# Attention softmax step: where the transposes and the two parts of the tile before stand in the order of work

## The chip, the cores and the metric

The kernel runs on one core of a Trainium2 chip. The core has five engines with a queue each: PE (TensorE, matrix products), DVE (VectorE), ACT (ScalarE), POOL (GpSimd) and SP (SyncE, which here issues DMAs). An engine works through its queue in order; engines wait for each other by semaphores. The metric is the device time of one execution in microseconds (us).

## The reference

Three stages in float32:

```python
q_pool = q.reshape(B, H, S // 2, 2, D).mean(axis=3)        # B 2, H 8, S 1152, D 64
scores = scale * q_pool @ k.T
attn = exp(scores - max(scores)); attn /= sum(attn) + 1e-9
x = (attn @ v) as [1152 tokens, 512]
xn = x / sqrt(mean(x * x) + 1e-6) * rms_g
y = (silu(xn @ w_gate) * (xn @ w_val)) @ w_out             # 512 -> 1536 -> 512
h = y @ w_in2;  out = (h * tanh(softplus(h))) @ w_out2     # 512 -> 2048 -> 512
```

## The kernel before

To keep float32's precision with 16-bit matrix products, each operand is kept as a high part (the value rounded to float16) and a low part (what the rounding left), and products are summed over the parts.

The attention runs first, in 72 steps: 8 pairs of heads (the code's groups g) of 9 tiles each, a tile being 128 pooled query rows. `attn_step(n)` writes out, in the order of its calls, what each engine gets for step n. This order is final: the kernel runs under a manual schedule, so every engine takes its instructions in exactly the order in which the calls issue them, and the framework only adds the waits for data and for free buffers. One tile passes through these calls:

- `scores(n)` (L237): PE multiplies queries and keys, 6 matmuls of 384 columns into one of two PSUM buffers of tile `s`.
- `row_max(n)` (L259): DVE takes the maximum of each row out of PSUM (L262, written to tile `m`) and scales it (L263).
- `row_exp(n)` (L266): ACT computes the exponential of 1152 columns from PSUM into `e` (float32, three buffers), L269.
- The exponentials have to be transposed and split into high and low parts, as tile `et` (five buffers), to be the weights of the product with v. Columns are divided: the first 640 go by DMA, the last 512 by PE.
  - DMA way: `split_hi` (ACT, L282) and `split_lo` (POOL, L134 of the helper `lo_op`) make the parts as `hl` (four buffers); `flip` (L292) has SP issue a transposing DMA from `hl` into `et`.
  - PE way: `flip_pe` (L297) transposes four blocks of `e` into one PSUM tile `ep`, of which there is a single buffer; `part_hi` (ACT, L309) writes the high part into `et`; `part_lo` (DVE, L314 by way of L134) reads `ep` and the high part and writes the low part, after which `ep` is free.
- `attn_v(n)` (L318), five steps later (LAG): PE multiplies `et` and v into `av`, a single PSUM buffer that two tiles share; `attn_r` and `attn_x` (L343, L353) are four small DVE operations that scale the rows, run for about every second tile. For the last pair of heads of a batch, `rms_sum` adds a sum of squares on ACT (L449).

`each(n, engine)` (L654) spreads the preparation of the next pair of heads over the nine steps of this one. By the position j of a step within its nine: on POOL `kv_scale` of k at j = 0 and of v at j = 6 (L141), low parts and the work on q in the others; on ACT `kv_hi` at j = 1, 2, 7, 8 (L154) and `q_hi` at 5 (L178); on PE `kq_flip` at j = 3, 4, 6, 7, 8 (L198), transposes into the PSUM buffer that the scores of step n - 1 have left, and on DVE `kq_keep` (L203), which copies them out of it, so that the scores of step n + 1 can have that buffer; the loads are issued from ACT's queue. The last pair of heads (steps 63 to 71) has no such work.

From step 46 on the steps of the rms norm of the first batch are mixed in, one after each attention step; from step 57 on, at odd steps, weight jobs (`job_step`, L420), which turn loaded weights into two parts: one ACT operation, three DVE operations (L396, L398, L400), one ACT and one POOL operation. Then the two feed-forward stages follow, on PE above all.

The part of `attn_step` that the change touches stands at L695 to L715.

Of the kernel before, what the change touches and what calls it, by code (L numbers as in the profile page):

```python
# [40 lines left out]
def kernel(  # L41
# [71 lines left out]
    def load(w, g, i, eng=nc.scalar):  # L113

        if g >= NPR:
            return
        b, h0 = g // NP, 2 * (g % NP)
        if i == 0:
            nat[w, g] = nat_p.tile([128, 2, NJ, D] if w != "q" else [128, NTI, 2, D], F32, tag="nat", name=w + "n")
        t = nat[w, g]  # L120
        nm = NI * 128 * 2
        if w != "q":
            eng.dma_start(out=t[:, i], in_=(k if w == "k" else v)[b, h0 + i].rearrange("(p j) d -> p j d", j=NJ))
        elif i < 2:
            eng.dma_start(
                out=t[:, i * NI:(i + 1) * NI], in_=q[b, h0 + i, 0:nm, :].rearrange("(p i r) d -> p i r d", i=NI, r=2))
        else:
            for e in range(2):
                eng.dma_start(out=t[e * TL:(e + 1) * TL, 2 * NI],
                                  in_=q[b, h0 + e, nm:, :].rearrange("(p r) d -> p r d", r=2))  # L130

    def lo_op(eng, out_, in_, s, hi):
        if isinstance(s, float) and s == 1.0:
            eng.tensor_tensor(out=out_, in0=in_, in1=hi, op=ALU.subtract)  # L134
        else:
            eng.scalar_tensor_tensor(out=out_, in0=in_, scalar=s, in1=hi, op0=ALU.mult, op1=ALU.subtract)  # L136

    def kv_scale(w, g):

        t = nat[w, g].rearrange("p h j d -> p (h j d)")  # L140
        nc.gpsimd.tensor_scalar(out=t, in0=t, scalar1=QK_S if w == "k" else V_S, scalar2=None, op0=ALU.mult)  # L141

    def kv_hi(w, g, e):
        if e == 0:
            if w == "k":
                cvt["k", g] = cv_p.tile([128, 2 * NJ, 2 * D], F16, tag="khl", name="khl")
            else:
                t = kq_p.tile([128, 2 * NJ, 2 * D + 2], F16, tag="vv", name="vv")
                nc.gpsimd.memset(t[:, :, 2 * D:2 * D + 1], 1.0)
                vvt[g] = t  # L150
        t = (cvt["k", g] if w == "k" else vvt[g])[:, e * NJ:(e + 1) * NJ, :]
        o = 0 if w == "k" else D
        sc = 1.0 if g else QK_S if w == "k" else V_S
        nc.scalar.activation(out=t[:, :, o:o + D], in_=nat[w, g][:, e], func=ACTF.Copy, scale=sc)  # L154

    def kv_lo(w, g, e):
        t = (cvt["k", g] if w == "k" else vvt[g])[:, e * NJ:(e + 1) * NJ, :]
        o = 0 if w == "k" else D
        sc = 1.0 if g else QK_S if w == "k" else V_S
        lo_op(nc.gpsimd if g else nc.vector, t[:, :, D - o:2 * D - o], nat[w, g][:, e], sc, t[:, :, o:o + D])  # L160
        if e == 1:
            del nat[w, g]

    def q_add(g):
        a = nat.pop(("q", g))
        s = cv_p.tile([128, NTI, D], F32, tag="qs", name="qs")
        (nc.gpsimd if g else nc.vector).tensor_tensor(out=s, in0=a[:, :, 0, :], in1=a[:, :, 1, :], op=ALU.add)
        cvt["s", g] = s
# [5 lines left out]
    def q_hi(g):  # L174

        t = cv_p.tile([128, NTI, 3, D], F16, tag="qhl", name="qhl")
        a = cvt["s", g]
        nc.scalar.activation(out=t[:, :, 0:3:2, :], in_=a.unsqueeze(2).to_broadcast([128, NTI, 2, D]), func=ACTF.Copy)  # L178
        cvt["q", g] = t
# [50 lines left out]
    def where(n):  # L230

        g, j = divmod(n, NTI)
        return g // NP, g, (j if g < NPR - 1 else (j - 1) % NTI)

    s_t, e_t, hl_t, et_t, av_t = {}, {}, {}, {}, {}

    def scores(n):  # L237
        b, g, j = where(n)
        kt = kqT[g][:, 0:2 * NJ, :]
        qt = kqT[g][:, 2 * NJ:, :]  # L240
        ps = ps_s.tile([128, SC, 512], F32, tag="s", name="s")
        heads = [(j % 2, j % 2 * NI + j // 2, 0, 128)] if j < 2 * NI else [
            (e, 2 * NI, e * TL, TL) for e in range(2)]
        per = SN // 128
        for c in range(SC):
            for e, slot, p0, m in heads:
                for w in range(2):
                    nc.tensor.matmul(  # L248
                        out=ps[p0:p0 + m, c, 0:SN],
                        lhsT=qt[:, w * NTI + slot, p0:p0 + m],  # L250
                        rhs=kt[:, e * NJ + c * per:e * NJ + (c + 1) * per, :].rearrange("p j t -> p (j t)"),
                        start=(w == 0),
                        stop=(w == 1),
                    )
        s_t[n] = ps
# [10 lines left out]
    def row_exp(n):  # L266
        ps, m = s_t.pop(n), mx.pop(n)
        e = e_p.tile([128, S], F32, tag="e", name="e")
        nc.scalar.activation(  # L269
            out=e.rearrange("p (c s) -> p c s", c=SC), in_=ps[:, :, 0:SN], func=ACTF.Exp,  # L270
            bias=m[:, 1:2], scale=s_scale)
        e_t[n] = e
        read[n] = ps
# [3 lines left out]
    def split_hi(n):  # L277

        if n < 0:
            return  # L280
        t = et_p.tile([128, 2, NB * 128], F16, tag="hl", name="hl", bufs=4)
        nc.scalar.activation(out=t[:, 0, :], in_=e_t[n][:, 0:NB * 128], func=ACTF.Copy)  # L282
        hl_t[n] = t

    def split_lo(n):
        e, t = e_t[n], hl_t[n]
        lo_op(nc.vector if n in LO_DVE else nc.gpsimd, t[:, 1, :], e[:, 0:NB * 128], 1.0, t[:, 0, :])

    def flip(n):
        t = hl_t.pop(n)  # L290
        r = et_p.tile([128, 2 * NJ, 128], F16, tag="et", name="et")
        nc.sync.dma_start_transpose(out=r[:, 0:2 * NB], in_=t.rearrange("p w s -> p (w s)"))  # L292
        et_t[n] = r
# [3 lines left out]
    def flip_pe(n):  # L297

        if n < 0:
            return  # L300
        e = e_t.pop(n)
        ps = ps_t.tile([128, PB, 128], F32, tag="t", name="ep")
        for s in range(PB):
            nc.tensor.transpose(out=ps[:, s, :], in_=e[:, (NB + s) * 128:(NB + s + 1) * 128], identity=idf)  # L304
        ep_t[n] = ps

    def part_hi(n):
        if n >= 0:
            nc.scalar.activation(out=et_t[n][:, 2 * NB:2 * NB + PB, :], in_=ep_t[n], func=ACTF.Copy)  # L309

    def part_lo(n):
        if n >= 0:
            r = et_t[n]
            lo_op(nc.vector, r[:, 2 * NB + PB:, :], ep_t.pop(n), 1.0, r[:, 2 * NB:2 * NB + PB, :])  # L314

    xb = {}
# [337 lines left out]
    def each(n, engine):  # L654

        g, j = n // NTI + 1, n % NTI
        if g >= NPR:
            return
        if engine == "load":
            if j in (0, 2):  # L660
                load("v", g, j // 2)
            elif j in (3, 4):
                load("k", g + 1, j - 3)
            elif j >= 6:
                load("q", g + 1, j - 6)
        elif engine == "act":
            if j in (1, 2):
                kv_hi("k", g, j - 1)
            elif j == 5:
                q_hi(g)  # L670
            elif j in (7, 8):
                kv_hi("v", g, j - 7)
        elif engine == "pool":
            if j in (0, 6):
                kv_scale("v" if j else "k", g)
            elif j in (1, 2):
                kv_lo("k", g, j - 1)
            elif j == 3:
                q_add(g)
            elif j == 4:  # L680
                q_scale(g)
            elif j == 5:
                q_lo(g)
            else:
                kv_lo("v", g, j - 7)
        elif j in FJ:
            f = FL[FJ.index(j)]
            if engine == "pe":
                kq_flip(read[n - 1], g, *f)
            else:  # L690
                kq_keep(g, f[0])
# [2 lines left out]

    def attn_step(n):  # L695
        scores(n)
        each(n, "pe")
        split_hi(n - 1)
        each(n, "act")
        row_max(n)  # L700
        each(n, "dve")
        row_exp(n)
        if n:
            split_lo(n - 1)
            flip(n - 1)
        each(n, "pool")
        each(n, "load")
        if n >= LAG:
            attn_v(n - LAG)
            attn_r(n - LAG)  # L710
            attn_x(n - LAG)
        flip_pe(n - 1)
        part_hi(n - 1)
        part_lo(n - 1)
        read.pop(n - 1, None)  # L715

    with tc.manual_schedule():
# [67 lines left out]
        for step in TAIL:  # L785
# [5 lines left out]
            else:  # L791
                n = NIT - LAG + int(step)
# [113 lines left out]
```

## Time and profile before

| what | value |
|---|---|
| time, median of 3 runs (lowest, highest) | 758.8 us (757.59, 759.13) |
| profiled execution: time, span | 757.44 us, 755.6 us |
| busy share of the span: PE, DVE, ACT, POOL | 83%, 62%, 51%, 47% |
| first and last exponential of the attention start at | 17.27 us, 332.73 us |
| mean granted TensorE clock | 0.959 of full |
| chain that ended last: PE, DVE, no visible wait, ACT | 41%, 31%, 13%, 9% |
| transposing DMAs `et` from `hl`: count, median from issue to landing | 72, 4.3 us |

The span is the time from the first to the last instruction of the profiled execution. "Busy" leaves out waiting; it is an average over stages that differ: in the attention no engine is full, while PE is nearly full later. A group of instructions in the profile has a source line, an engine, an operation and its tiles (written <- read); L134 is the helper for all low parts, so its groups are told apart by tile. An engine's idle time before a group is put down to what released it last. Times in the timeline are start and duration; on DVE, ACT and POOL the record of an instruction can overlap the next by about 0.1 us, so distances between starts are also used.

### The profile page before, as it was taken

The numbers are of one execution on the slowest core, as the hardware profiler recorded it, in microseconds if no ns is written. First come the engines' busy times: TensorE is split into PE (matmuls) and PEld (weight loads), VectorE is DVE, ScalarE is ACT, GpSimd is POOL, SyncE is SP. The second block draws the span as 40 slices with busy tenths as digits, with TensorE's granted clock in tenths as the row PEclk, the third lists the DMA queues.
The fourth block names the chain that finished last, engine by engine and source line by source line (L and its number), as shares of the span: only waits on it lengthen the run. The fifth ranks groups of instructions, "written<-read, shape, count | busy, mean of one in ns | idle before, by whom it ended". The sixth has DMA issues, their size and how long they took to land.

```text
span 755.6 us, 13340 instructions
## 1 busy us (share of the span) xinstructions
PE 629.6 (83%) x5232; PEld 441.1 (58%) x5232; DVE 465.9 (62%) x769; ACT 385.0 (51%) x654; POOL 355.6 (47%) x271
## 2 busy tenths in 40 slices
PE   3767677767657747578999999999999999999997
PEld 2555555545546545456777777777775555555553
DVE  5577777666677787865599998128939981111110
ACT  4766766676756655464555555304426652222321
POOL 2786878776868872320577777304504330000000
PEclk9799999999998986869999999999999999999999
DMA  5656666655658873431454555014514410000101
GB/s 176 139 123 136 125 129 133 142 108 120 134 119 186 139 150 79 111 70 36 120 159 150 159 168 162 7 56 140 168 57 144 167 53 28 15 1 1 43 0 43
DMA packets 143471, 79.25 MB, mean 105 GB/s; under 512 B 106288, under 2 KB 133936, under 8 KB 143408
## 3 DMA queue, kind: packets, MB, share of 16 engines
q1 hardware_dynamic: 132752, 63.00, 33.9%
q10 hardware_dynamic: 10656, 15.40, 8.0%
q8 instruction: 41, 0.67, 0.4%
q14 instruction: 22, 0.18, 0.1%
HBM read 50.07 MB, written 2.36 MB: 69 GB/s over the span
## 4 chain that ended last, share of the span: by engine, by line
PE 41%; DVE 31%; issue 13%; ACT 9%; POOL 3%; ACTq 1%; DMA 1%; SPq 0%; DVEq 0%; POOLq 0%
DVE m L262 10%; DVE c L398 6%; DVE et L134 5%; ACT et L309 5%; PE z L507 4%; PE z L509 4%; PE z L508 4%; PE po L644 4%; PE po L642 4%; PE po L643 4%; PE py L507 3%; PE py L509 3%; PE py L508 3%; DVE c L396 3%; ACT e L269 2%
## 5 line engine op out<-in xcount | busy, mean ns | idle before, releaser
L134 POOL TENSOR_TENSOR hl<-e,hl 128x640 f16<-128x640 f32 x71 | 101.1, 1424 | 92.9 <-ACT hl L282 71.3
L269 ACT ACTIVATE e<-s,m 128x1152 f32<-128x1152 f32 x72 | 87.8, 1220 | 104.1 <-DVE m L263 79.6
L248 PE MATMUL s<-kqT 128*128 128x384 f16 (+1 forms) x480 | 90.6, 350 | 43.3 <-DVE kqT L203 39.7
L134 DVE TENSOR_TENSOR et<-ep,et 128x512 f16<-128x512 f32 x72 | 49.8, 692 | 86.4 <-ACT et L309 86.4
L262 DVE TENSOR_REDUCE m<-s 128x1 f32<-128x1152 f32 x72 | 97.1, 1348 | 0.8 <-PE s L248 0.8
L331 PE MATMUL av<-vv,et 128*128 128x129 f16 (+1 forms) x720 | 79.8, 230 | 20.9 <-DVE x L366 17.2
L136 DVE SCALAR_TENSOR_TENSOR g<-mo,g 128x384 f16<-128x384 f32 x48 | 26.9, 562 | 100.5 <-ACT g L617 100.5
L248 PEld LDWEIGHTS <-kqT 128*128 128x128 f16 (+1 forms) x480 | 46.8, 106 | 71.5 <-issue 54.9
L331 PEld LDWEIGHTS <-et 128*128 128x128 f16 (+1 forms) x720 | 69.9, 105 | 29.8 <-issue 28.6
L398 DVE SCALAR_TENSOR_TENSOR c<-gx,c 128x512 int32<-128x512 int32 x68 | 79.1, 1164 | 2.3
L134 POOL TENSOR_TENSOR stretch<-c,stretch 128x512 f16<-128x512 f32 x40 | 51.4, 1284 | 58.9 <-ACT stretch L407 58.8
L333 PE MATMUL av<-vv,et 128*128 128x65 f16 (+1 forms) x720 | 77.6, 201 | 0.0
L400 DVE SCALAR_TENSOR_TENSOR c<-raw,c 128x512 int32<-128x512 int32 x68 | 75.1, 1105 | 2.3
L304 PE MATMUL ep<-idf,e 128*128 128x128 f32 x288 | 51.2, 305 | 26.2 <-DVE et L134 24.1
L333 PEld LDWEIGHTS <-et 128*128 128x128 f16 (+1 forms) x720 | 68.3, 105 | 1.0 <-issue 0.5
L134 POOL TENSOR_TENSOR h<-fo,h 128x288 f16<-128x288 f32 x48 | 48.8, 1017 | 42.3 <-ACT h L544 42.3
L507 PE MATMUL z<-y,w2i 128*128 128x384 f16 x192 | 62.6, 326 | 0.0
L509 PE MATMUL z<-y,w2i 128*128 128x384 f16 x192 | 62.6, 326 | 0.0
L508 PE MATMUL z<-y,w2i 128*128 128x384 f16 x192 | 62.6, 326 | 0.0
L611 ACT ACTIVATE mo<-z 128x384 f32<-128x384 f32 x48 | 23.2, 483 | 71.3 <-PE z L509 71.3
L507 PE MATMUL pv<-stretch 128*128 128x288 f16 x192 | 55.7, 290 | 2.4 <-DVE fo L537 2.3
L507 PE MATMUL pg<-stretch 128*128 128x288 f16 x192 | 55.9, 291 | 1.9 <-DMA stretch<-xh 1.9
(98 smaller groups left out, 1542.9 us busy)
## 6 DMA issues: line engine op xcount, KB each, us to landing
raw<-in_moe_w_out_dram SPq DMA_DIRECT2D x28, 512.0 KB, 3.4
raw<-in_moe_w_in_dram SPq DMA_DIRECT2D x16, 512.0 KB, 3.7
raw<-in_moe_w_gate_dram SPq DMA_DIRECT2D x8, 512.0 KB, 3.7
raw<-in_moe_w_val_dram SPq DMA_DIRECT2D x8, 512.0 KB, 3.6
vn<-in_v_dram ACTq DMA_DIRECT2D x14, 288.0 KB, 3.5
kn<-in_k_dram ACTq DMA_DIRECT2D x12, 288.0 KB, 3.4
qn<-in_q_dram ACTq DMA_DIRECT2D x12, 256.0 KB, 3.2
raw<-in_moe_w_gate_dram ACTq DMA_DIRECT2D x4, 512.0 KB, 5.0
```

The source lines that it names most:

```text
L134: eng.tensor_tensor(out=out_, in0=in_, in1=hi, op=ALU.subtract)
L248: nc.tensor.matmul(out=ps[p0:p0 + m, c, 0:SN], lhsT=qt[:, w * NTI + slot, p0:p0 + m], rhs=kt[:, e * NJ + c * per:e * NJ + (c + 1) * per, : ...
L262: nc.vector.tensor_reduce(out=m[:, 0:1], in_=ps[:, :, 0:SN], op=ALU.max, axis=AXL.XY, negate=True)
L269: nc.scalar.activation(out=e.rearrange("p (c s) -> p c s", c=SC), in_=ps[:, :, 0:SN], func=ACTF.Exp, bias=m[:, 1:2], scale=s_scale)
L304: nc.tensor.transpose(out=ps[:, s, :], in_=e[:, (NB + s) * 128:(NB + s + 1) * 128], identity=idf)
L331: nc.tensor.matmul(out=av[0:m, o0:o0 + 2 * D + 1], lhsT=et[:, z, p0:p0 + m], rhs=vr[:, 0:2 * D + 1], start=(jj == 0), stop=False)
L333: nc.tensor.matmul(out=av[0:m, o0 + D:o0 + 2 * D + 1], lhsT=et[:, z + (NB if jj < NB else PB), p0:p0 + m], rhs=vr[:, D:2 * D + 1], start=F ...
L398: nc.vector.scalar_tensor_tensor(out=c, in0=gi, scalar=-0x80000000, in1=c, op0=ALU.bitwise_and, op1=ALU.bitwise_or)
L400: nc.vector.scalar_tensor_tensor(out=c, in0=t[:, :, :, 0], scalar=29, in1=c, op0=ALU.logical_shift_right, op1=ALU.bitwise_or)
L507: nc.tensor.matmul(out=ps, lhsT=w0, rhs=x0, start=(i == 0), stop=False)
L508: nc.tensor.matmul(out=ps, lhsT=w0, rhs=x1, start=False, stop=False)
L509: nc.tensor.matmul(out=ps, lhsT=w1, rhs=x0, start=False, stop=(i == n - 1))
```

## The change

The calls of `attn_step` are put in another order; no instruction is added, removed or altered. Within step n, `flip_pe(n - 1)` moves from the end of the step to directly behind `scores(n)`, ahead of `kq_flip` and `attn_v` on PE. `split_lo(n - 1)` and `flip(n - 1)` are called earlier, which leaves POOL's and SP's order as it was. `part_hi(n - 1)` moves on ACT from behind the exponential of n to directly behind `split_hi(n - 1)`, ahead of `kv_hi` or `q_hi` and of the exponential of n. `part_lo(n - 1)` moves on DVE from the end of the step to directly behind `kq_keep`, ahead of `attn_r` and `attn_x`. The tile `e` is let go of in `part_lo` rather than in `flip_pe`, since `split_lo` now comes after `flip_pe`.

```diff
     def flip_pe(n):
...
-        e = e_t.pop(n)
+        e = e_t[n]
...
     def part_lo(n):
         if n >= 0:
             r = et_t[n]
+            del e_t[n]
             lo_op(nc.vector, r[:, 2 * NB + PB:, :], ep_t.pop(n), 1.0, r[:, 2 * NB:2 * NB + PB, :])
...
     def attn_step(n):
         scores(n)
+        flip_pe(n - 1)
         each(n, "pe")
         split_hi(n - 1)
+        if n:
+            split_lo(n - 1)
+            flip(n - 1)
+        part_hi(n - 1)
         each(n, "act")
         row_max(n)
         each(n, "dve")
+        part_lo(n - 1)
         row_exp(n)
-        if n:
-            split_lo(n - 1)
-            flip(n - 1)
         each(n, "pool")
         each(n, "load")
         if n >= LAG:
             attn_v(n - LAG)
             attn_r(n - LAG)
             attn_x(n - LAG)
-        flip_pe(n - 1)
-        part_hi(n - 1)
-        part_lo(n - 1)
         read.pop(n - 1, None)
```

## Rows read from the trace of the kernel before

**Rows 1.** Costliest groups: busy and mean ns of one, idle time before and its releaser.
```profile
L134 DVE TENSOR_TENSOR et<-ep,et 128x512 f16<-128x512 f32 x72 | 49.8, 692 | 86.4 <-ACT et L309 86.4
```

**Rows 2.** Chain of waits, one step: start us, us, what.
```profile
111.86 0.17 DVE m L263
112.11 0.37 ACT e L269
...
113.23 0.60 ACT et L309
113.85 0.69 DVE et L134
```

**Rows 3.** Timeline of DVE, the same step: start us, us, engine, line, operation.
```profile
111.93 0.68 DVE L203 COPY kqT<-s 128x1024 f16<-128x1024 f16 x1
112.53 0.15 DVE L350 TENSOR_SCALAR r<-av 128x2 f32<-128x2 f32 x1
...
113.24 0.29 DVE L366 TENSOR_TENSOR x<-av,r 128x128 f32<-128x128 f32 x1
...
114.45 1.35 DVE L262 TENSOR_REDUCE m<-s 128x1 f32<-128x1152 f32 x1
115.84 0.15 DVE L263 TENSOR_SCALAR m<-m 128x1 f32<-128x1 f32 x1
```

**Rows 4.** Timeline of ACT: exponentials of steps 0, 9, 18, 45, 63 and 71.
```profile
17.27 1.22 ACT L269 ACTIVATE e<-s,m 128x1152 f32<-128x1152 f32 x1 [1.80 <-DVE m L263]
...
52.15 1.22 ACT L269 ACTIVATE e<-s,m 128x1152 f32<-128x1152 f32 x1 [1.67 <-DVE m L263]
...
88.22 1.22 ACT L269 ACTIVATE e<-s,m 128x1152 f32<-128x1152 f32 x1 [1.67 <-DVE m L263]
...
200.82 1.22 ACT L269 ACTIVATE e<-s,m 128x1152 f32<-128x1152 f32 x1 [1.67 <-DVE m L263]
...
287.98 1.22 ACT L269 ACTIVATE e<-s,m 128x1152 f32<-128x1152 f32 x1 [1.80 <-PE av L333]
...
332.73 1.22 ACT L269 ACTIVATE e<-s,m 128x1152 f32<-128x1152 f32 x1 [1.67 <-PE av L333]
```

**Rows 5.** Windows: us, busy PE, PEld, DVE, ACT, POOL; PEclk, DMA share, GB/s.
```profile
52.00:88.00 36.00, 25.31 (x313) 19.45 (x312) 25.88 (x53) 24.66 (x32) 27.78 (x20) 1.00 0.61 132
...
288.00:333.00 45.00, 29.66 (x282) 22.58 (x280) 32.45 (x54) 23.37 (x35) 14.90 (x11) 0.80 0.42 94
```

**Rows 6.** Timeline of PE: attn_v, flip_pe, scores; scores and kq_flip.
```profile
105.70 0.22 PE L331 MATMUL av<-vv,et 128*128 128x129 f16 x1
...
106.64 0.66 PE L304 MATMUL ep<-idf,e 128*128 128x128 f32 x4
107.13 1.14 PE L248 MATMUL s<-kqT 128*128 128x384 f16 x6
...
112.66 1.14 PE L248 MATMUL s<-kqT 128*128 128x384 f16 x6 [1.39 <-DVE kqT L203]
113.63 0.61 PE L198 MATMUL s<-ident,qhl 128*128 128x128 f16 x8
```

**Rows 7.** Timeline of ACT: split_hi and a kv_hi that waits for POOL.
```profile
53.74 0.74 ACT L282 ACTIVATE hl<-e 128x640 f16<-128x640 f32 x1
55.08 0.68 ACT L154 ACTIVATE khl<-kn 128x576 f16<-128x576 f32 x1 [0.60 <-POOL kn L141]
```

**Rows 8.** Timeline of POOL: split_lo and kv_scale at position 0.
```profile
86.63 1.40 POOL L134 TENSOR_TENSOR hl<-e,hl 128x640 f16<-128x640 f32 x1 [1.61 <-ACT hl L282]
88.00 3.13 POOL L141 TENSOR_SCALAR kn<-kn 128x1152 f32<-128x1152 f32 x1
```

**Rows 9.** Timeline of DVE: first operations of two weight jobs, and a row maximum.
```profile
267.06 0.42 DVE L396 TENSOR_SCALAR c<-gx 128x512 int32<-128x512 int32 x1
...
290.33 1.40 DVE L396 TENSOR_SCALAR c<-gx 128x512 int32<-128x512 int32 x1
...
294.17 1.35 DVE L262 TENSOR_REDUCE m<-s 128x1 f32<-128x1152 f32 x1
```

## The prediction

> **What bounds the kernel now.** I read the page's costliest groups first, then the chain of waits inside the attention, then the timeline of each engine over one step. In the groups the reader is to see an engine that waits inside a step: DVE stands idle 86.4 us in front of its 72 part_lo, all of it until ACT's part_hi (L309) [rows 1]. The chain shows where that wait lies, in a ring: row maximum of tile n, exponential of n, then part_hi and part_lo of n - 1, then the row maximum of n + 1 [rows 2, 3]. No data asks for the middle link: row_max(n + 1) stands behind part_lo(n - 1) in DVE's order, and that waits for part_hi(n - 1), which stands behind exp(n) in ACT's order. From start to start the ring is 1.39 (row maximum to L263) + 0.25 (to the exponential) + 1.12 (to part_hi) + 0.62 (to part_lo) + 0.60 (to the next maximum) = 3.98 us [rows 2, 3]. A group of nine steps takes 88.22 - 52.15 = 36.07 us; steps 0 to 45 take 183.55, steps 45 to 63 87.16, steps 63 to 71 44.75 [rows 4]. In a stretch of about one group DVE is busy 25.9 us, ACT 24.7, POOL 27.8 and PE 25.3 [rows 5]. So nothing is full; order sets the time.
>
> **The change part by part.** No instruction is added or removed. POOL's and SP's own orders, each queue's loads and the transposing DMA stay in sequence; three things move.
>
> *part_lo(n - 1) on DVE*, from behind attn_x to in front of attn_r, and no longer behind exp(n). Its 86.4 us of idle time go, up to what is late next. DVE's own work per step, start to start, is 1.39 + 0.07 + 0.60 = 2.06 us, plus 0.60 for kq_keep (five steps of nine, the last shorter) and 0.95 for attn_r and attn_x (five of nine) [rows 3]: 2.9 us on the mean.
>
> *part_hi(n - 1) on ACT*, from behind exp(n) to in front of it. This adds a wait: exp(n) now stands behind part_hi(n - 1), which waits for PE's flip_pe(n - 1), which waits for exp(n - 1). split_hi follows exp directly and reads its output, so it starts 1.22 (the exponential's duration) + 0.04 (my estimate of a handoff) later, not 1.12. flip_pe takes 0.66 beside split_hi's 0.74 [rows 6, 7]. So part_hi starts 2.00 after its tile's exponential, the next exponential 2.48 after it at the earliest, with 0.58 more in four steps (kv_hi) and 1.08 more in one (q_hi).
>
> *flip_pe(n - 1) on PE*, in front of kq_flip and attn_v(n - 5), which now wait for exp(n - 1) as well, with scores(n + 1) and attn_x behind them. PE, start to start: scores 0.97, flip_pe 0.49, attn_v 0.87 to 0.94 (0.87 taken), kq_flip about 0.5 of its 0.61 [rows 6]. From scores' start to the row maximum I take their 1.14 + 0.10.
>
> What is late next I worked through one group, time zero at the row maximum of its step 0, the exponential before at -1.12 (the state that repeats).
> Steps 0 and 1: POOL sets it. split_hi ends at 0.98 (exp -1, + 1.36 behind two small load issues, + 0.74), POOL's split_lo takes 1.37 and kv_scale 3.13, to 5.5 [rows 8]; kv_hi on ACT waits for it, as it does by 0.60 us now [rows 7]. exp(1) starts at 6.13 instead of 4.37, which the row maximum before it would allow. Row maxima: 0, 2.74, 5.81.
> Step 2: exp(1) + 1.27 flip_pe, + 0.48 attn_v, + 0.87 scores, + 1.24: row maximum 3 at 9.99; exp(2), behind the second kv_hi, at 9.19.
> Steps 3 and 4: DVE sets it. Step 3: kq_keep waits for kq_flip until 11.63, then 0.60 + 0.61 + 0.95: 13.79. Step 4: 2.06 + 0.60 + 0.95 = 3.61: 17.40.
> Step 5: flip_pe(4) at 17.00, attn_v, scores: 19.59; exp(5) behind q_hi at 19.29.
> Step 6: kq_flip follows exp(5), kq_keep at 21.73: 23.89.
> Step 7: scores wait for kq_keep: 27.31; exp(7) waits for POOL's second kv_scale, 26.5.
> Step 8: part_lo waits for part_hi(7) until 29.12, + 0.61 + 0.95 = 30.68, with exp(8) at 29.56, so the state repeats. Group: 30.7 us against 36.07.
>
> Sum. Steps 0 to 45: 5 x 30.7 + 1.8 for the five sum-of-squares steps (ACT waits there for attn_x; now they cost about 4) = 155, against 183.5: 28 us. Steps 45 to 63: what now exceeds two groups, 87.16 - 72.1 = 15.0 us (rms steps, first weight jobs, mostly DVE's), stays; 2 x 5.4 = 10.7 us saved. Steps 63 to 71, no kq or kv work: DVE's 8 x 2.06 + 5 x 0.95 + three jobs of 3.84 [rows 9] = 32.8; I take 35, since TensorE's granted clock has a mean of 0.80 there [rows 5]: 9.5 us saved. Behind the loop about 0.5 us is won, and the rest moves rigidly: its first units need weights whose jobs run by step number in the loop. Together 48 to 49 us. The profiled execution took 757.44 us (span 755.6), so 709; the median of the runs shown is 758.8, 1.4 higher, which gives **711 us**.
>
> Bounds of what the trace doesn't show. exp beside row_max of the next tile, both reading PSUM: never so now. Nearest rows: kq_keep and attn_x read PSUM beside an exponential and take the 0.68 and 0.29 of other steps [rows 3], so I take 0; the other end is full serialisation, 1.22 per step (a rival below). Handoffs: 0.04 to 0.10 taken, from L263's end to the exponential's start, 0.1; at twice that the ring of two steps over PE has five of them, +0.2 per step, 14 us. Denser transfers: the DMA share of 0.61 [rows 5] becomes 0.72, et has four steps of slack; 0. Below nothing: fewer stalls may keep the clock up in steps 59 to 71, at most the 2 us I put in.
>
> A weight job's first DVE operation took 0.42 us in the first job and 1.40 in the third, which lasted 3.84 up to the next row maximum [rows 9]. The Trainium skill ("SBUF — State Buffer", Who interferes with whom) has the pair of ports that VectorE and GpSimd share as an exclusive lock: the second to issue waits for the whole of the other's instruction. The trace agrees for the jobs. A denser POOL would then hit the first job too, three operations by 1 us each, and four more operations of the rms steps: 718 by that rule, inside the forecast's own range; the sum above keeps the jobs' present cost.
>
> **The rivals.**
> *POOL's floor.* The waits overlap better than in my table and only POOL's 27.8 us per group are left [rows 5]: 3 us per group more over seven groups, 690. For: POOL queues four tiles deep. Against: kv_hi needs kv_scale a step later, already a wait now.
> *PE's ring is longer.* Every second-step handoff over exp, flip_pe, kq_flip, kq_keep, scores costs more than taken, 0.3 us per step: 71 x 0.3 = 21 us, 732. For: scores already wait for kq_keep in each such step. Against: that handoff is short now.
> *The gain is given back.* The order is new but the stage after the loop waits for the same weights: 757 to 760. Against: loads are issued by step number, DMA is at 0.61 [rows 5].
> *Slower: exp and row_max serialise.* Place: DVE and ACT on PSUM at once. Lengthening of y per step gives a group of 26.0 + 9y on DVE; it exceeds 36.07 from y = 1.12. At 1.22: 37.0, eight groups, 7 us more than before: 766. Against: rows 3, as said.
> *Slower: half clock.* PE's in-order work is 0.97 + 0.49 + 0.94 + 5/9 x 0.5 = 2.68 us per step at the full clock; with a share x of it at 1.2 GHz it is 2.68 (1 + x), over 3.98 from x = 0.5. At x = 0.6 it is 4.29, 71 x 0.31 = 22 us more than before: 781. For: a mean of 0.80 in steps 63 to 71, where PE idles under DVE's jobs. Against: 1.00 in the regular groups with PE busy 25.3 of 36 us [rows 5], and the same work will fill 30.7.
>
> **How the numbers follow.** Forecast 0.60 (702 to 722), POOL's floor 0.12, longer ring 0.17, given back 0.03, serialise 0.04, half clock 0.04. Leaving out the outer half of POOL's floor, the worst of the longer ring and the three last, the range is 694 to 738. A change under 0.2%, 1.5 us, can't be told from none. Faster: 0.60 + 0.12 + 0.17 = 0.89; same 0.03; slower 0.08.
>
> **What would show it.** Right: DVE's idle time before part_lo falls from 86.4 to under 15 us; row maxima run beside the exponential before; a regular group takes about 30.7 us with the long steps where kv_hi waits for kv_scale; exp waits for POOL in steps 1 and 7. Wrong: exponential or row maximum longer than 1.22 and 1.35; PE's clock below 1.00 in the regular groups; idle time before flip_pe or scores of over 1 us in most steps; or a stage after the loop that grew.

## The result and the profile after

The changed kernel takes **698.0 us** (median of 4 runs, 696.74 to 699.07) where the kernel before took 758.45 beside it (757.59 to 759.13): a ratio of 0.9203, with an interval of 0.9183 to 0.9223. Four more runs of the same kernel, in a later series, gave a median of 698.41 and again a ratio of 0.9203 (0.9171 to 0.9236). The forecast was 711, with a range of 694 to 738. The profiled execution took 697.47 us, with a span of 695.7 (before: 757.44 and 755.6); its mean granted TensorE clock is 0.983 of full (before: 0.959).

First the costliest groups of the kernel after: busy us and mean ns of one, then the idle time before them and what ended it. In this kernel part_lo stands at L134, the exponential at L269 and the row maximum at L262, as before; from L314 on, lines have moved down by one.

```profile
L262 DVE TENSOR_REDUCE m<-s 128x1 f32<-128x1152 f32 x72 | 97.2, 1350 | 12.5 <-PE s L248 12.2
L269 ACT ACTIVATE e<-s,m 128x1152 f32<-128x1152 f32 x72 | 87.4, 1214 | 20.3 <-DVE m L263 20.2
L134 DVE TENSOR_TENSOR et<-ep,et 128x512 f16<-128x512 f32 x72 | 49.4, 686 | 14.9 <-ACT et L309 14.5
```

DVE's idle time before part_lo fell from 86.4 us [rows 1] to 14.9, and neither of the two operations that now run beside each other on PSUM (row maximum and exponential, as at 83.50 and 83.75 us below) became longer by more than 2 ns of its mean.

The timeline of ACT of the kernel after (start, duration, operation; in brackets the idle time and what ended it) shows the exponentials of steps 0, 18, 27, 45, 63 and 71, and between them the new order as far as the exponential of step 19, with ACT's two waits for POOL in that group:

```profile
17.54 1.22 ACT L269 ACTIVATE e<-s,m 128x1152 f32<-128x1152 f32 x1 [1.81 <-DVE m L263]
...
79.37 1.22 ACT L269 ACTIVATE e<-s,m 128x1152 f32<-128x1152 f32 x1 [0.23 <-DVE m L263]
80.62 0.74 ACT L282 ACTIVATE hl<-e 128x640 f16<-128x640 f32 x1
81.34 0.60 ACT L309 ACTIVATE et<-ep 128x512 f16<-128x512 f32 x1
83.16 0.68 ACT L154 ACTIVATE khl<-kn 128x576 f16<-128x576 f32 x1 [1.23 <-POOL kn L141]
83.75 1.20 ACT L269 ACTIVATE e<-s,m 128x1152 f32<-128x1152 f32 x1
...
103.40 0.68 ACT L154 ACTIVATE vv<-vn 128x576 f16<-128x576 f32 x1 [1.16 <-POOL vn L141]
...
109.95 1.22 ACT L269 ACTIVATE e<-s,m 128x1152 f32<-128x1152 f32 x1 [0.39 <-DVE m L263]
...
172.77 1.22 ACT L269 ACTIVATE e<-s,m 128x1152 f32<-128x1152 f32 x1 [0.23 <-DVE m L263]
...
246.02 1.22 ACT L269 ACTIVATE e<-s,m 128x1152 f32<-128x1152 f32 x1 [0.62 <-DVE m L263]
...
276.43 1.21 ACT L269 ACTIVATE e<-s,m 128x1152 f32<-128x1152 f32 x1
```

Put beside [rows 4], the starts say where the 59.9 us of span went:

| stretch | before | after | saved | forecast to save |
|---|---|---|---|---|
| start to step 0 | 17.27 | 17.54 | -0.3 | 0 |
| steps 0 to 45 | 183.55 | 155.23 | 28.3 | 28 |
| steps 45 to 63 | 87.16 | 73.25 | 13.9 | 10.7 |
| steps 63 to 71 | 44.75 | 30.41 | 14.3 | 9.5 |
| from step 71 to the end | 422.9 | 419.3 | 3.6 | 0.5 |

A regular group (steps 18 to 27) takes 109.95 - 79.37 = 30.58 us; the table of the prediction said 30.7. The five groups of steps 0 to 45 took 29.90, 31.93, 30.58, 30.52 and 32.30 us (the last with the five sum-of-squares steps, for which the prediction had 32.5). The row maxima of that group, in the timeline of DVE after, test the table step by step:

```profile
77.74 1.35 DVE L262 TENSOR_REDUCE m<-s 128x1 f32<-128x1152 f32 x1
...
80.30 1.36 DVE L262 TENSOR_REDUCE m<-s 128x1 f32<-128x1152 f32 x1 [0.42 <-PE s L248]
...
83.50 1.35 DVE L262 TENSOR_REDUCE m<-s 128x1 f32<-128x1152 f32 x1
...
87.47 1.36 DVE L262 TENSOR_REDUCE m<-s 128x1 f32<-128x1152 f32 x1 [0.45 <-PE s L248]
...
91.38 1.35 DVE L262 TENSOR_REDUCE m<-s 128x1 f32<-128x1152 f32 x1
...
94.95 1.34 DVE L262 TENSOR_REDUCE m<-s 128x1 f32<-128x1152 f32 x1
...
97.13 1.36 DVE L262 TENSOR_REDUCE m<-s 128x1 f32<-128x1152 f32 x1
...
101.42 1.35 DVE L262 TENSOR_REDUCE m<-s 128x1 f32<-128x1152 f32 x1
...
104.84 1.36 DVE L262 TENSOR_REDUCE m<-s 128x1 f32<-128x1152 f32 x1 [0.66 <-PE s L248]
...
108.32 1.35 DVE L262 TENSOR_REDUCE m<-s 128x1 f32<-128x1152 f32 x1
```

From 77.74 on they come at 0, 2.56, 5.76, 9.73, 13.64, 17.21, 19.39, 23.68, 27.10 and 30.58; the table had 0, 2.74, 5.81, 9.99, 13.79, 17.40, 19.59, 23.89, 27.31 and 30.68.

What is late in the place of the old ring is read from the waits of the kernel after over the attention (17 to 285 us; total us, times, longest):

```profile
PE ep L304 <- ACT e L269: 42.6, 42, 3.3
...
DVE et L134 <- ACT et L309: 14.5, 15, 2.1
...
ACT et L309 <- PE ep L304: 10.9, 23, 1.6
ACT khl L154 <- POOL kn L141: 8.4, 6, 1.7
```

No one engine took over. PE waits 42 times, one microsecond on the mean, for the exponential (the link that the table had on purpose: flip_pe(n - 1) stands right behind the exponential), and ACT waits for POOL's scaling of k at the start of each group that prepares the next. In windows of the kernel after (us; busy PE, PEld, DVE, ACT, POOL; granted clock; DMA share; GB/s) all four are fuller than in [rows 5] without being full, the granted clock of steps 18 to 45 stays at 1.00, and that of the last nine steps rose from 0.80 to 0.94:

```profile
79.00:110.00 31.00, 25.38 (x322) 19.87 (x320) 26.42 (x55) 25.84 (x34) 28.45 (x20) 1.00 0.81 153
172.77:246.02 73.25, 54.09 (x634) 41.95 (x633) 65.57 (x121) 56.49 (x76) 67.15 (x45) 0.93 0.88 168
246.02:276.43 30.41, 22.69 (x273) 17.12 (x271) 27.77 (x54) 23.78 (x34) 14.62 (x12) 0.94 0.68 139
276.00:286.00 10.00, 8.85 (x105) 7.36 (x102) 5.11 (x16) 5.57 (x11) 1.40 (x1) 1.00 0.37 71
```

Of steps 9 to 45, those up to 18 are the exception. There the granted clock has a mean of 0.95 (0.62 from 53 to 57 us), where it was 1.00 before [rows 5], and one `scores` in PE's timeline takes nearly twice its usual 1.14 us:

```profile
55.20 2.11 PE L248 MATMUL s<-kqT 128*128 128x384 f16 x6
```

PE had waited 2.20 us just before, at flip_pe, for an exponential that stood behind POOL's scaling, and about 3 us of work then ran at the lower of the clock's two levels (1.2 instead of 2.4 GHz). The group took 31.93 us, 1.35 more than the next, and did so in the later series too. What lowered the clock is not shown: in the next group PE waited 1.94 us at the same place and the clock stayed at 1.00.

### The profile page after: what moved, and what is told of

It is laid out like the page before. It is cut to its first block, busy times and chain, and to the rows that moved or that the text cites. A ratio compares the mean times of both kernels' runs of the same rounds, so it can differ in the third digit from the quotient of the medians.

```text
span 695.7 us, 13395 instructions
## 1 busy us (share of the span) xinstructions
PE 611.0 (88%) x5232; PEld 430.4 (62%) x5232; DVE 460.0 (66%) x769; ACT 391.1 (56%) x654; POOL 357.5 (51%) x271
## 4 chain that ended last, share of the span: by engine, by line
PE 47%; DVE 20%; POOL 11%; issue 11%; ACT 8%; DMA 2%; SPq 0%; ACTq 0%; POOLq 0%; DVEq 0%
DVE c L399 6%; PE z L508 4%; PE z L510 4%; PE z L509 4%; PE po L645 4%; PE po L644 4%; PE po L643 4%; ACT e L269 3%; PE py L508 3%; PE py L510 3%; PE py L509 3%; POOL hl L134 3%; DVE m L262 3%; DVE c L397 3%; DVE c L401 2%
## 5 line engine op out<-in xcount | busy, mean ns | idle before, releaser
L134 POOL TENSOR_TENSOR hl<-e,hl 128x640 f16<-128x640 f32 x71 | 101.1, 1423 | 36.3 <-ACT hl L282 24.4
L262 DVE TENSOR_REDUCE m<-s 128x1 f32<-128x1152 f32 x72 | 97.2, 1350 | 12.5 <-PE s L248 12.2
L248 PE MATMUL s<-kqT 128*128 128x384 f16 (+1 forms) x480 | 87.5, 340 | 16.6 <-DVE kqT L203 14.2
L269 ACT ACTIVATE e<-s,m 128x1152 f32<-128x1152 f32 x72 | 87.4, 1214 | 20.3 <-DVE m L263 20.2
L304 PE MATMUL ep<-idf,e 128*128 128x128 f32 x288 | 47.8, 290 | 45.3 <-ACT e L269 42.6
L134 POOL TENSOR_TENSOR stretch<-c,stretch 128x512 f16<-128x512 f32 x40 | 52.5, 1313 | 55.1 <-ACT stretch L408 55.1
L401 DVE SCALAR_TENSOR_TENSOR c<-raw,c 128x512 int32<-128x512 int32 x68 | 77.2, 1135 | 2.3
L399 DVE SCALAR_TENSOR_TENSOR c<-gx,c 128x512 int32<-128x512 int32 x68 | 75.6, 1112 | 2.3
L332 PE MATMUL av<-vv,et 128*128 128x129 f16 (+1 forms) x720 | 75.3, 224 | 1.2 <-DVE x L367 1.2
L304 PEld LDWEIGHTS ep<-idf,e 128*128 128x128 f32 x288 | 33.8, 146 | 66.5 <-ACT e L269 61.0
L334 PE MATMUL av<-vv,et 128*128 128x65 f16 (+1 forms) x720 | 73.2, 195 | 0.0
L332 PEld LDWEIGHTS <-et 128*128 128x128 f16 (+1 forms) x720 | 66.5, 101 | 3.5 <-issue 1.9
L134 POOL TENSOR_TENSOR h<-fo,h 128x288 f16<-128x288 f32 x48 | 48.7, 1016 | 37.0 <-ACT h L545 37.0
L248 PEld LDWEIGHTS <-kqT 128*128 128x128 f16 (+1 forms) x480 | 42.1, 103 | 39.3 <-issue 21.7
L334 PEld LDWEIGHTS <-et 128*128 128x128 f16 (+1 forms) x720 | 65.5, 102 | 0.4
L134 DVE TENSOR_TENSOR et<-ep,et 128x512 f16<-128x512 f32 x72 | 49.4, 686 | 14.9 <-ACT et L309 14.5
```

Of the source, the lines that this page charges most:

```text
L248: nc.tensor.matmul(out=ps[p0:p0 + m, c, 0:SN], lhsT=qt[:, w * NTI + slot, p0:p0 + m], rhs=kt[:, e * NJ + c * per:e * NJ + (c + 1) * per, : ...
L262: nc.vector.tensor_reduce(out=m[:, 0:1], in_=ps[:, :, 0:SN], op=ALU.max, axis=AXL.XY, negate=True)
L269: nc.scalar.activation(out=e.rearrange("p (c s) -> p c s", c=SC), in_=ps[:, :, 0:SN], func=ACTF.Exp, bias=m[:, 1:2], scale=s_scale)
L332: nc.tensor.matmul(out=av[0:m, o0:o0 + 2 * D + 1], lhsT=et[:, z, p0:p0 + m], rhs=vr[:, 0:2 * D + 1], start=(jj == 0), stop=False)
L334: nc.tensor.matmul(out=av[0:m, o0 + D:o0 + 2 * D + 1], lhsT=et[:, z + (NB if jj < NB else PB), p0:p0 + m], rhs=vr[:, D:2 * D + 1], start=F ...
L399: nc.vector.scalar_tensor_tensor(out=c, in0=gi, scalar=-0x80000000, in1=c, op0=ALU.bitwise_and, op1=ALU.bitwise_or)
```

## The experiments

The first three undo one engine's part of the change each and keep the other two.

**PE's order of before.** flip_pe(n - 1) goes back behind kq_flip and attn_v.

```diff
         scores(n)
-        flip_pe(n - 1)
         each(n, "pe")
+        if n >= LAG:
+            attn_v(n - LAG)
+        flip_pe(n - 1)
...
         if n >= LAG:
-            attn_v(n - LAG)
             attn_r(n - LAG)
```

> PE's order of before (kq_flip, attn_v, then flip_pe), ACT's and DVE's order of the changed kernel. Theory 1 (the gain needs all of exp, flip_pe, part_hi in one piece): flip_pe now waits behind attn_v, and attn_v behind the attn_x of the step before, so part_hi comes 0.9 us or more later in most steps and exp behind it; the hand table of one group then gives about 36.2 us instead of 30.7, so 740 to 755 in all. Theory 2 (only ACT's and DVE's order matter, PE has slack): 698 plus or minus 5.

Measured: 732.59 us, ratio 0.9656 (0.9628 to 0.9685). A regular group takes 122.18 - 86.44 = 35.74 us (about 36.2 expected), and steps 0 to 45 take 179.0: 4.5 us of the 28 are left. The total came out below the range expected, since steps 45 to 63 (79.8) and 63 to 71 (36.05) keep more than half of what they had won; I had put the loss of the regular steps on all of them. The rows are the exponentials at both ends of a group, in ACT's timeline of this kernel:

```profile
86.44 1.22 ACT L269 ACTIVATE e<-s,m 128x1152 f32<-128x1152 f32 x1
...
122.18 1.22 ACT L269 ACTIVATE e<-s,m 128x1152 f32<-128x1152 f32 x1
```

and its waits over the attention:

```profile
ACT et L309 <- PE ep L304: 63.0, 52, 2.4
DVE et L134 <- ACT et L309: 45.6, 53, 2.2
...
PE av L332 <- DVE x L367: 31.6, 19, 4.3
```

The reader is to see that the wait has moved along the ring rather than gone: part_hi stands ahead of the exponential, so the exponential waits for flip_pe, and flip_pe stands behind an attn_v that waits for attn_x to free `av`.

**ACT's order of before.** part_hi goes back behind the exponential; part_lo has to follow it in program order.

```diff
-        part_hi(n - 1)
         each(n, "act")
         row_max(n)
         each(n, "dve")
-        part_lo(n - 1)
         row_exp(n)
+        part_hi(n - 1)
+        part_lo(n - 1)
```

> part_hi(n - 1) back behind exp(n) on ACT; PE's and DVE's order of the changed kernel. Theory 1 (what breaks the ring is part_hi in front of exp): the ring of 3.98 us stays, and attn_r and attn_x, 0.95 us in five steps of nine, now stand behind part_lo inside it, so slower than before: 40 x 0.95 = 38 us more, 785 to 797. Theory 2 (the gain comes from part_lo's place on DVE): about 700.

Measured: 786.19 us, ratio 1.0355 (1.0318 to 1.0393). The chain of waits of this kernel, one step (start, us, what), is the old ring with a piece more in it:

```profile
100.42 0.07 ACT e L269
...
101.54 0.60 ACT et L309
...
102.16 0.69 DVE et L134
...
103.48 0.29 DVE x L367
...
103.78 1.27 DVE m L262
...
105.32 0.39 ACT e L269
```

From exponential to exponential it is 105.32 - 100.42 = 4.90 us: the 3.98 of before and 0.92 for attn_r and attn_x, which DVE had done beside the exponential [rows 3] and which now stand behind a part_lo that waits. So the ring does not break without ACT's move, and the moves on PE and DVE without it are a loss. No run made one of the three moves alone.

**DVE's order of before.** part_lo(n - 1) goes from behind kq_keep to the end of the step, behind attn_x.

```diff
-        part_lo(n - 1)
         row_exp(n)
...
             attn_x(n - LAG)
+        part_lo(n - 1)
```

> part_lo(n - 1) back behind attn_r and attn_x on DVE; PE's and ACT's order of the changed kernel. Theory 1: most of the gain stays; part_lo up to 0.95 us later frees the single buffer ep later and holds flip_pe in steps 4 and 5 of a group, group 32.3 instead of 30.7, so 707 to 713. Theory 2 (part_lo's place on DVE carries the gain): 730 or more.

Measured: 704.1 us, ratio 0.9283 (0.9251 to 0.9314). The group is 111.77 - 79.67 = 32.10 us (32.3 expected). Two rows, of PE's and of DVE's timeline in this kernel, show the extra 1.5 us in one step of the group (5.42 instead of 3.87): flip_pe waits for the single `ep`, which part_lo frees late; then DVE waits with attn_r for PE's attn_v.

```profile
91.71 0.63 PE L304 MATMUL ep<-idf,e 128*128 128x128 f32 x4 [0.60 <-DVE et L134]
```

```profile
94.53 0.15 DVE L351 TENSOR_SCALAR r<-av 64x2 f32<-64x2 f32 x1 [0.90 <-PE av L334]
```

So, with the other two moves in place, DVE's is worth 6 us of the 60.

**POOL's scaling of k and v left out**, in the changed kernel and in the one before.

```diff
             if j in (0, 6):
-                kv_scale("v" if j else "k", g)
+                pass
```

> The changed kernel without POOL's kv_scale for all but the first pair of heads (k and v stay unscaled there; nothing else is left out). Theory 1 (POOL's kv_scale sets two waits of each group, the rest is set by DVE, ACT and the PE ring): exp of step 1 of a group starts 1.44 us earlier, group 29.2 instead of 30.7, 686 to 690. Theory 2 (POOL's 27.8 us of work are the floor of the loop): falls to DVE's 26 us per group, 670 or less. Theory 3 (kv_hi's wait is covered): 698.

> The kernel before, without POOL's kv_scale for all but the first pair of heads (k and v stay unscaled there). Theory 1 (POOL's wait became a limit only through the change; before, the ring covered it): 758 plus or minus 1.5. Theory 2 (POOL's kv_scale always cost its share): about 10 us less, 748.

Measured: the changed kernel 686.14 us, ratio 0.9041 (0.9014 to 0.9067), 12 us under the kernel after; the kernel before 756.86, ratio 0.9974 (0.9953 to 0.9995), with regular steps of 3.97 to 4.01 as ever. The 12 us lie in steps 0 to 45 (155.23 to 148.35) and in steps 45 to 63 (73.25 to 67.32). The same 6 us of POOL per group are worth 1.36 us per group in the new order (window of the first kernel, one group) and next to nothing in the old one:

```profile
76.84:106.06 29.22, 24.88 (x314) 19.44 (x312) 26.00 (x53) 25.47 (x32) 21.70 (x18) 1.00 0.79 164
```

With POOL at 21.7 of 29.22 us, the group is still 3 us above the fullest engine, DVE; the rest is put down to the handoffs between PE, ACT and DVE, which no run singled out.

**The weight jobs' waits for POOL.** In the kernel before, the low parts of the four weight jobs in the loop and those of tiles 61, 63, 65 and 67 are made by DVE, so that POOL is idle beside the jobs of steps 63, 65 and 67; beside that of step 61 it still has a low part of v.

```diff
-LO_DVE = (71,)
+LO_DVE = (61, 63, 65, 67, 71)
...
+        for x in jobs[:NE]:
+            x["eng"] = nc.vector
```

> The kernel before, with POOL kept out of the stretch of the weight jobs: the low parts of the four jobs that finish in the loop and of tiles 61, 63, 65 and 67 go to DVE (0.7 to 0.8 us each there, the tiles' beside the exponential). Theory 1 (the jobs' DVE operations were slow because POOL held the shared ports): they fall to 0.42, 0.69 and 0.69, a job from 3.84 to 1.8 plus its 0.7, four jobs give 5 us: 752 to 755. Theory 2 (they were slow for another reason): their durations stay, 758 to 761.

Measured: 752.65 us, ratio 0.9918 (0.9886 to 0.9951); a job's step goes from 7.85 to 6.37 us. The costliest groups of DVE in this kernel, 260 to 325 us:

```profile
L400 DVE SCALAR_TENSOR_TENSOR c<-raw,c 128x512 int32<-128x512 int32 x5 | 4.5, 899 | 0.2
L398 DVE SCALAR_TENSOR_TENSOR c<-gx,c 128x512 int32<-128x512 int32 x5 | 3.5, 692 | 0.2
...
L396 DVE TENSOR_SCALAR c<-gx 128x512 int32<-128x512 int32 x5 | 2.1, 420 | 0.0
```

and of the kernel before, over the same stretch:

```profile
L398 DVE SCALAR_TENSOR_TENSOR c<-gx,c 128x512 int32<-128x512 int32 x5 | 7.8, 1552 | 0.2
L396 DVE TENSOR_SCALAR c<-gx 128x512 int32<-128x512 int32 x5 | 6.0, 1203 | 0.0
```

What L398 and L396 took over 692 and 420 ns was waiting for POOL. L400 has a mean of 875 ns before and of 899 here: four of its five took 0.69 us, and the one of step 61 took 1.72, beside POOL's low part of v, which began 0.05 us before it. The Trainium skill ("SBUF — State Buffer", Who interferes with whom) says that the engine which issues first keeps the shared pair of ports for its whole instruction; the durations agree.

**Towards a faster kernel.** Three versions build on the changed one. The first scales k and v in halves, one head at a time, so that kv_hi of the first head waits for 1.6 us of POOL and not for 3.1. The second also starts the rms norm's steps at 54 instead of 46; the third, instead, has five products `xn` of the rms norm made by DVE.

```diff
-    def kv_scale(w, g):
+    def kv_scale(w, g, e):
-        t = nat[w, g].rearrange("p h j d -> p (h j d)")
+        t = nat[w, g][:, e].rearrange("p j d -> p (j d)")
...
+            if j in (0, 1, 6, 7):
+                kv_scale("v" if j > 5 else "k", g, j % 6)
             if j in (0, 6):
-                kv_scale("v" if j else "k", g)
+                pass
```

> The changed kernel with each kv_scale cut into its two heads, at steps 0 and 1 (k) and 6 and 7 (v), so that the first kv_hi waits for half of it and the second for the other half a step later; all work is kept. Theory 1 (the wait for kv_scale costs, not POOL's sum of work): the same as without kv_scale, group 29.2, 686 to 689. Theory 2 (POOL's 27.8 us of work per group, or the halves' own overhead, hold the loop): 694 to 699.

Measured: 692.73 us, ratio 0.9142 (0.9103 to 0.918), between the two theories. The regular group went to 29.18 us as the first had it, the same as with no scaling at all; steps 45 to 63 won nothing (72.93 against 73.25, where leaving the scaling out had given 67.3), and steps 63 to 71 took 31.88, 1.5 more than in the changed kernel. The window of those steps shows POOL and DVE both busy 68 of 73 us:

```profile
165.16:238.09 72.93, 52.93 (x620) 40.86 (x619) 67.95 (x120) 55.96 (x76) 67.57 (x49) 0.92 0.83 169
```

```diff
-RMS0 = 46
+RMS0 = 54
```

> The kernel with halved kv_scale, and the rms steps of the first batch begun at step 54 instead of 46, so that four of their five POOL products fall in steps 60 to 66 or just before, where the next pair's k and v work ends. Theory 1 (in steps 45 to 63 the halves gain nothing because POOL carries the rms products and weight parts there on top of 27.8 us a group): steps 45 to 63 fall from 72.9 to about 69, steps 63 to 71 grow by about 2, 690 to 691. Theory 2 (DVE's weight jobs alone set that stretch): no change, 692 to 693.

Measured: 690.55 us, ratio 0.9102 (0.9071 to 0.9134). Steps 45 to 63 go to 69.56, as expected, steps 63 to 71 rise by 1.5 to 33.4. The total's lead over the first version (2.2 us) lies inside the spread of the runs. The 3.4 us have a second reading that was not tested: the three DVE operations of step 59's weight job, which meet POOL, took 5.88 us in the first version and 2.77 here.

```diff
-            (nc.gpsimd if b == 0 else nc.vector).tensor_tensor(
+            nc.vector.tensor_tensor(
...
```

> The kernel with halved kv_scale, and the five rms products (1.3 us each on POOL) on DVE instead, about 0.7 us each. Theory 1 (POOL is late in steps 45 to 63): steps 45 to 63 fall by about 3 us, 689 to 690. Theory 2 (DVE sets that stretch): 3 us more, 695 to 696.

Measured: 691.81 us, ratio 0.912 (0.9082 to 0.9158), runs from 689.59 to 694.53: inconclusive in the total, since neither the first version nor the second can be told from it. Its profiled execution, the slowest of the four, doesn't show the fall by 3 us of the first theory: steps 45 to 63 took 74.60 us, and three of the five products took 1.15 to 1.77 us on DVE, where 0.7 was expected. The first two of these versions beat the changed kernel by 5 and 7 us.

The changed kernel itself ran again beside the first version; its 698.41 us stand in the section on the result:

> The changed kernel as it is, on the same chip as the three others, for their comparison: 698 plus or minus 1.5.

## Why the prediction was right, and where its sizes were off

**The ring** was as read: DVE's wait before part_lo was order, not data. Taking back ACT's part alone brings the 3.98 us back, and more. The measured 698.0 lies all the same 4 us below the 702 to 722 to which the prediction gave 0.60; the sizes that were off follow.

**What is late next** was right step by step in the regular groups (30.58 and 30.52 us against 30.7). That steps 0 to 45 took 155.23 against 155 is in part luck: the first group was 0.8 us shorter than the table, and the second 1.2 longer, with the stretch at the lower clock in it. Its three setters each showed: POOL's scaling in steps 1 and 7 (ACT's waits of 1.23 and 1.16 us; without the scaling 1.36 us less per group), PE's link over flip_pe (undone, 35.74 per group), and DVE's order (undone, 32.10).

**Unknown costs taken at nothing.** The exponential and the row maximum side by side take 1214 and 1350 ns (1.22 and 1.35 us before), so the rival of serialising falls. The transposing DMA lands after a median of 3.7 us, not later than before (4.3), at a DMA share of 0.81 where I had 0.72. The granted clock stays at 1.00 in steps 18 to 45, so the rival of half clock, priced at 22 us more than before, falls; but half clock did come in steps 9 to 18, for about 3 us, and with it one of the signs of being wrong. Another sign was badly put: idle time of about 1 us before flip_pe in most steps was to mean that the forecast is wrong, but the working itself has flip_pe waiting for the exponential; 42 such waits, of 1.0 us on the mean, came with the forecast group. POOL's floor (a group of 27.8 us), a longer ring of PE (0.3 us per step) and a stage after the loop that takes the gain back did not come either: the groups took 30.5 us, and the stage behind the loop became shorter.

**Terms that were mis-sized** make up the 11 us between the 48.7 us forecast to be saved and the 59.9 measured:

- *Three weight jobs of 3.84 us each, kept.* They took 1.78, 1.79 and 3.71, 4.2 us less. Before, POOL's low part of a weight tile began at 290.28 us, 0.05 ahead of DVE's first operation at 290.33, which then took 1.40 [rows 9]. After, in step 63, the timeline of DVE shows the job done before POOL's next operation:

```profile
246.46 0.42 DVE L397 TENSOR_SCALAR c<-gx 128x512 int32<-128x512 int32 x1
246.91 0.69 DVE L399 SCALAR_TENSOR_TENSOR c<-gx,c 128x512 int32<-128x512 int32 x1
247.63 0.69 DVE L401 SCALAR_TENSOR_TENSOR c<-raw,c 128x512 int32<-128x512 int32 x1
248.24 1.35 DVE L262 TENSOR_REDUCE m<-s 128x1 f32<-128x1152 f32 x1
```

and the timeline of POOL the operations on either side:

```profile
244.70 1.40 POOL L134 TENSOR_TENSOR hl<-e,hl 128x640 f16<-128x640 f32 x1 [1.12 <-ACT hl L282]
...
247.84 1.50 POOL L134 TENSOR_TENSOR stretch<-c,stretch 128x512 f16<-128x512 f32 x1 [1.74 <-ACT stretch L408]
```

  The job of step 67 meets POOL again (1.53 and 1.77 us for its last two operations). The prediction weighed these meetings as a loss alone; a new order can break up a meeting as well as make one.
- *The rms steps' 15.0 us, kept.* Three operations on 128 x 5 elements (L466 to L468 of before) took 1.30, 1.20 and 1.18 us, each beside another operation of POOL's (the low parts of `hl` and `qhl`, the product `xn`); after, 1.30, 0.17 and 0.17, 2.0 us less. The two weight jobs in these steps went both ways. The three operations of step 61's took 4.76 us before and 2.86 after. Those of step 59's, 1.80 before, took 4.84 beside a denser POOL, the loss that the prediction named and left out of its sum:

```profile
226.07 2.38 DVE L397 TENSOR_SCALAR c<-gx 128x512 int32<-128x512 int32 x1
```

  Together these make 0.9 of the 3.2 us that steps 45 to 63 gained beyond the forecast; the other 2.3 I can't put to a place.
- *2.2 us for the clock in steps 63 to 71.* With the jobs as they came out, DVE's sum is 32.8 - 4.2 = 28.6, and 30.41 was measured: 1.8 of the 2.2 were used, though the granted clock rose to 0.94. Which wait holds them the runs did not single out. (The 9.5 us saved are 44.75 - 35 = 9.75; with this and the rest unrounded the prediction's own terms give 709.6, not 711.)
- *Behind the loop 0.5 us*, measured 3.6. From the last exponential to the first product of the feed-forward stage it was 336.12 - 332.73 = 3.39 us and is 278.19 - 276.43 = 1.76: 1.6 us, 0.4 of them in a flip_pe that ran at the lower clock before. The first unit's 24 products followed each other every 0.24 us before, for 17 of them, which is half clock (the granted clock of 333 to 343 us was 0.66), and every 0.12 after (1.00 in the last of the windows above): 4.97 us to 2.95, 2 us from the clock. Beside it, PE's idle time just before flip_pe here fell from 2.55 to 0.96 us; that this is the cause was not tested on its own.

**The range** held by 4 us at its low end, and that end had been drawn for half of POOL's floor, which did not come: the number lies in the range for other reasons than those it was drawn for. The terms above were priced at their present cost rather than bounded below, though the trace had the shorter durations of the same operations (0.42 us in the first job).

## What to carry to other kernels

Where engines work through their queues in a written order, look in the chain of waits for a link that no data asks for, follow the whole ring, and move its parts together: here the moves on PE and DVE without ACT's lost 3.5%, and without PE's 4.5 of 28 us were left in steps 0 to 45. Then work the next limit out step by step over one period, each queue in its order; the table of nine steps was right to 0.12 us in 30.6 where the granted clock was 1.00. And price waits between two engines that share a resource from both sides, since moving work moves the meetings too; an engine's load that cost nothing under the old ring (POOL's scaling, 0.26%) can be worth 12 us under the new order, so look at the old dead ends again.

## What was not expected of the hardware

- A meeting of DVE with POOL cost a tiny operation as much as a large one: 1.20 and 1.18 us instead of 0.17 for 128 x 5 elements, and 1.40 instead of 0.42 for 128 x 512 int32, where POOL had begun 0.05 us earlier.
- The granted clock of the last nine steps of the attention rose from 0.80 to 0.94 with no operation of PE's changed, only the waits between them; in steps 9 to 18 it fell for a short stretch in the faster kernel.
- ACT's split_hi, which reads what the exponential just wrote, starts 1.25 us after the exponential's start (80.62 - 79.37); an ACT operation behind it that doesn't read it started after 1.12 [rows 2].
